# Seven-product weight sums, made in the second batch's up phase instead of the first batch's feed-forward part

## The chip, the cores and the metric

The kernel runs on one core of a Trainium2 chip. The metric is the device time of one execution in microseconds (us), the median of several. The engines are TensorE (PE, matmuls; its weight loads are listed as PEld), VectorE (DVE), ScalarE (ACT) and GpSimd (POOL). SyncE (SP) issues all DMA transfers, in the order of its queue.

## The reference

Attention with a window and block summaries, then a feed-forward part in which the tokens are first mixed by a matrix of rank 32. Cut to what matters:

```python
batch, heads, S, D = 4, 8, 768, 64           # DM = 512, hidden DF = 2048
a = softmax([scores in a window of 16 | scores with the block maxima of k])
x = a @ [v | block means of v]               # -> (4, 768, 512)
u = x + ((x^T @ U) @ V)^T                    # U (768, 32), V (32, 768)
out = u + relu(u @ w_ch1) @ w_ch2            # w_ch1 (512, 2048), w_ch2 (2048, 512)
```

All weights reach the chip as float64 bit patterns and are turned into float32 there.

## The kernel before, in words

**Precision.** A matmul operand is held as a high part (ACT casts it, L184) and a low part (the rest, by a subtraction on POOL, L185; a few on DVE), and a product is three matmuls: high by high, high by low, low by high. Casting and subtracting together are called a split.

**Order.** Every engine works through its own list of instructions in the order in which the program's text issues them, and so does SP with its transfers. The order is written by hand: attention steps of the next batch are spread between the matmuls of the present one.

**First batch** (from some 57 to 236 us; before that its attention). The loop at L1024 runs over the 16 blocks `f` of 128 hidden columns, in two token halves `hf`. Each half does 12 matmuls of the up product (L791), the relu into `gh`, `gl` (L803, L804), and 9 matmuls of the down product (L813). Beside that, weights two or three blocks ahead are loaded as 512 KB of float64 words, turned into float32 by POOL (L160) and DVE (L166, L169), and split. `traffic` issues the transfers of each quarter of a block. The float32 weights are stored to DRAM for the later batches (`store_up`, `store_down`). The first batch's result leaves through `leave_rows` (L826: copies out of PSUM on ACT and, for one of three, DVE), transposes on PE (L834) and additions on DVE (L837, L838).

**Later batches.** Each has an up phase (1061 to 1130) and a down phase. The up product goes by pairs `p` of hidden blocks with seven products in place of eight: the 2 x 2 blocks A11, A12, A21, A22 of the weights and four sums of them, S1 to S4, meet seven operands made of the activations. Of a pair, the products use A11, A12, A22 and the four sums, each block 128 x 256. PE runs seven products of six matmuls (L1066) a pair; results leave PSUM by copies on ACT (L1088, L1100, L1112, L1125) and additions on DVE (L1092, L1105, L1126, the last at a pair's end). Between them stand the attention steps of the next batch: matmuls L321 and L423, masked scores on DVE (L341, written as operations with an accumulator `neg`), exponentials on ACT (L351), the largest keys per block on DVE (L286, copied by L303), and a turn of the exponentials by way of DRAM (`squares`, `there`, `at`: L371, L376, L384).

**Weights of the later batches.** `fetch_weight` (L744) loads the next 512 or 384 KB from DRAM into one of three tiles (`whole`), `prepare` (L751) splits the next unit of it into one of eight tiles (`parts`). The units of a pair are A (A11, A12), S0 (s2, s1), S1 (s3, s4) and D (A22). Units are split one pair ahead of their use. `tick` runs once a step and starts a due load.

**The sums before.** `sum_weights` (L701) makes them in the first batch, in two halves at every even `f`, from the two float32 tiles of the pair: L709 and L710 give s1 and s2, L712 and L713 give s3 and s4, each 128 x 256 on DVE. `store_sums` stores them (512 KB a pair). `store_up` stores all of A11, A12 (256 KB) and of the other tile only A22 (128 KB).

Of the kernel before, what the change touches and what calls it, by code (L numbers as in the profile page):

```python
# [84 lines left out]
def body(ctx: ExitStack, tc, q0, q1, k, v, vn, uv, w1, w2, mask, ident, rep, out):  # L85
# [28 lines left out]
    def hidden_place(k, dt=F32):  # L114
        return wt.tile([P, 4 * NH], dt, name="place", tag=f"h{k}")
# [561 lines left out]
    def by_parts(val):  # L677

        return val.rearrange("p (i k f) -> p k i f", k=2, f=P)
# [14 lines left out]

    w_kept, w_sums = {}, {}
    up_there = [dram.tile([P, 14 * P], F32, name=f"up{p}", bufs=1) for p in range(NF // 2)]
    down_there = [dram.tile([P, 2, DM], F32, name=f"down{p}", bufs=1) for p in range(NF // 2)]

    def sum_weights(p, n):  # L701

        a1, a2 = by_parts(w_kept[2 * p]), by_parts(w_kept[2 * p + 1])
        if n == 0:
            w_sums[p] = hidden_place(p % 2)[:, : 8 * P]
        sums = w_sums[p].rearrange("p (b i f) -> p b i f", b=4, f=P)
        s2, s1, s3, s4 = (sums[:, b] for b in range(4))
        if n == 0:
            nc.vector.tensor_tensor(s1, a2[:, 0], a2[:, 1], ALU.add)  # L709
            nc.vector.tensor_tensor(s2, s1, a1[:, 0], ALU.subtract)  # L710
        else:
            nc.vector.tensor_tensor(s3, a1[:, 0], a2[:, 0], ALU.subtract)  # L712
            nc.vector.tensor_tensor(s4, a1[:, 1], s2, ALU.subtract)  # L713
# [12 lines left out]

    def store_sums(p):
        nc.sync.dma_start(out=up_there[p][:, 4 * P : 12 * P], in_=w_sums[p])

    loads, units = [], []
    for _ in range(1, B):
        for p in range(NF // 2):
            loads += [up_there[p][:, : 8 * P], up_there[p][:, 8 * P :]]
            units += [("A", p), ("S0", p), ("S1", p), ("D", p)]
        for p in range(NF // 2):
            loads.append(down_there[p].rearrange("p t c -> p (t c)"))
            units += [("down", 2 * p), ("down", 2 * p + 1)]
    load_tags = ("w2", "w0_1", "w0_2")  # L740
    unit_tags = ("w1_1", "w0_3", "w1_2", "w0_4", "w1_3", "w0_0", "w1_4", "w1_0")
    fetched, prepared, used, due = [], [], [], []

    def fetch_weight():  # L744
        n = len(fetched)
        if n < len(loads):
            t = wt.tile([P, 2 * DM], F32, name="whole", tag=load_tags[n % 3])[:, : loads[n].shape[-1]]
            nc.sync.dma_start(out=t, in_=loads[n])
            fetched.append(t)

    def prepare():  # L751

        n = len(prepared)
        if n == len(units):
            return
        key = units[n]
        second = key[0] in ("S0", "D") or key[0] == "down" and key[1] % 2 == 1
        whole = fetched[n // 2][:, DM:] if second else fetched[n // 2][:, :DM]
# [9 lines left out]
        prepared.append((key, t))  # L768
# [220 lines left out]
    def traffic(f, i):  # L989
# [7 lines left out]
                fetch_weight()  # L997
        if i == 1:
            store_down(f)
            if f % 2:  # L1000
                store_sums(f // 2)
            if f == NF - 2:
                prepare()
        if i == 2:
            if 1 < f and f + RING - 2 < NF:
                load_weight(1, f + RING - 2)
            if f == NF - 4:
                fetch_weight()
            if f == NF - 1:
                prepare()  # L1010
# [13 lines left out]
    for f in range(NF):  # L1024
        for hf in range(2):
# [3 lines left out]
            if hf == 0:  # L1029
                if 0 < f:  # L1030
                    split_weights(f + 1)
                if f % 2 == 0:
                    sum_weights(f // 2, 0)
            elif f + 3 <= NF:
                scale_weights(f + 3)
            sum_values(4 * f + 2 * hf)
            run(turn, hf)
            if hf == 1 and f % 2 == 0:
                sum_weights(f // 2, 1)
            if prev is not None:  # L1040
                pf, phf, pg = prev
                if pf == 0:
# [265 lines left out]
```

## Time and profile before

| | us |
|---|---|
| median of 3 runs | 681.97 |
| lowest and highest | 680.58, 685.45 |
| the profiled execution | 678.02 |
| its span, first to last instruction | 676.2 |

| in the span | PE | DVE | ACT | POOL |
|---|---|---|---|---|
| busy, us | 641.9 | 386.6 | 343.1 | 372.0 |
| share | 95% | 57% | 51% | 55% |

The span runs from the first to the last instruction; times in rows of the profile are counted from its start. A row of the timeline gives start, length, engine, line, operation, output and inputs, and in brackets how long the engine stood idle before it and what ended that. L12 is line 12 of the kernel. Names like `place` and `whole` are tiles; `place` is used for many. The first batch's attention takes up to some 57 us, its feed-forward part up to 236, the second batch's up phase up to 307 and its down phase up to 387.

### The profile page before, as it was taken

To read this page: it belongs to the slowest core of one execution; us is meant where nothing else is said; L and a number is where in the kernel's file an instruction comes from. 1 tells how busy PE (TensorE), PEld (TensorE's weight loads), DVE (VectorE), ACT (ScalarE), POOL (GpSimd) and SP (SyncE) were. 2 spreads that over 40 slices of the span, in tenths; PEclk is the share of its full clock that TensorE was granted. 3 is DMA by queue.
4 is the path that set the end of the run, shared out by engine and by line. 5 is a ranking of instruction groups with operands and counts; after the bars stand their busy time and mean duration, and the time that the engine had idled before them with its cause. 6 is when DMAs were issued, how large, how long until landed. Compare 5 with 4: busy or idle time off the path is not lost.

```text
span 676.2 us, 13190 instructions
## 1 busy us (share of the span) xinstructions
PE 641.9 (95%) x4800; PEld 568.2 (84%) x4800; DVE 386.6 (57%) x1041; ACT 343.1 (51%) x751; POOL 372.0 (55%) x428
## 2 busy tenths in 40 slices
PE   5889997989999899999999999999999999999997
PEld 4768796879888799998877899998877899998886
DVE  3778798777898666555655634566654432232222
ACT  3855356355433556665453467665543365553322
POOL 5846967635697757651245486661334375563420
PEclk9999999899999999999999999999999999999999
DMA  9999679898992169785438059777432144431002
GB/s 250 249 345 279 218 231 297 252 272 305 279 330 100 52 185 309 209 250 151 143 104 248 23 174 311 229 222 220 127 97 79 55 148 165 139 126 62 32 0 94
DMA packets 82752, 124.47 MB, mean 184 GB/s; under 512 B 7680, under 2 KB 57728, under 8 KB 82688
## 3 DMA queue, kind: packets, MB, share of 16 engines
q1 hardware_dynamic: 82688, 123.63, 60.3%
q8 instruction: 38, 0.62, 0.4%
q14 instruction: 26, 0.21, 0.1%
HBM read 96.34 MB, written 27.26 MB: 183 GB/s over the span
## 4 chain that ended last, share of the span: by engine, by line
PE 75%; DMA 11%; DVE 6%; ACT 3%; SPq 2%; POOL 2%; issue 1%; ACTq 0%; POOLq 0%; DVEq 0%
PE acc L1151 27%; PE ps_h L1066 24%; PE acc L813 7%; PE ps_h L791 6%; PE ps_s L321 4%; PE ps_x L423 3%; DMA place<-in_q 2%; DMA qz<-in_q 2%; PE ps_o L610 2%; DMA place<-in_w 1%; DMA at<-there 1%; DMA place<-in_v 1%; DVE gl L1136 1%; DMA kt<-in_k 1%; DMA place<-in_k 1%
## 5 line engine op out<-in xcount | busy, mean ns | idle before, releaser
L185 POOL TENSOR_TENSOR parts<-whole,parts 128x512 fp32r<-128x512 f32 (+1 forms) x144 | 181.6, 1270 | 165.6 <-ACT parts L184 137.1
L1151 PE MATMUL acc<-parts,gh 128*128 128x512 f32 x576 | 193.4, 399 | 0.0
L1066 PE MATMUL ps_h<-op,parts 128*128 128x384 f32 x1008 | 188.4, 339 | 1.2 <-POOL parts L185 0.6
L1066 PEld LDWEIGHTS ps_h<-op,parts 128*128 128x128 f32 x1008 | 173.6, 188 | 3.1 <-POOL parts L185 0.9
L1151 PEld LDWEIGHTS acc<-parts,gh 128*128 128x128 f32 x576 | 108.1, 188 | 22.9 <-issue 0.8
L1151 PE MATMUL acc<-parts,gl 128*128 128x512 f32 x288 | 113.1, 393 | 1.9 <-DVE gl L1136 1.9
L1136 DVE SCALAR_TENSOR_TENSOR gl<-place,gh 128x768 fp32r<-128x768 f32 x48 | 58.9, 1228 | 83.1 <-ACT gh L1135 83.0
L184 ACT CAST parts<-whole 128x512 fp32r<-128x512 f32 (+1 forms) x144 | 83.5, 583 | 5.8 <-DMA whole<-up 4.3
L351 ACT ACTIVATE e<-e,neg 128x120 f32<-128x120 f32 x144 | 46.5, 386 | 59.7 <-DVE neg L341 53.6
L791 PE MATMUL ps_h<-place 128*128 128x384 f32 x384 | 74.3, 341 | 1.2 <-DVE place L592 0.5
L813 PE MATMUL acc<-place,gh 128*128 128x512 f32 x192 | 68.3, 411 | 2.1 <-POOL place L185 2.1
L791 PEld LDWEIGHTS ps_h<-place 128*128 128x128 f32 x384 | 66.6, 188 | 4.2 <-DVE place L592 1.3
L1135 ACT ACTIVATE gh<-place 128x768 fp32r<-128x768 f32 x48 | 40.6, 846 | 55.1 <-PE acc L1151 54.9
L1151 PEld LDWEIGHTS acc<-parts,gl 128*128 128x128 f32 x288 | 54.2, 188 | 13.1 <-DVE gl L1136 3.9
L160 POOL TENSOR_SCALAR val<-place 128x512 f32<-128x512 f32 (+1 forms) x30 | 48.7, 1638 | 29.6 <-ACT place L147 17.7
L185 POOL TENSOR_TENSOR place<-val,place 128x512 fp32r<-128x512 f32 x29 | 38.6, 1351 | 19.5 <-ACT place L184 19.5
L185 POOL TENSOR_TENSOR op<-tmp,op 128x384 fp32r<-128x384 f32 x24 | 24.5, 1030 | 42.7 <-ACT op L184 38.5
L341 DVE CUSTOM_DVE_ANT_0 e<-ps_s,mask_sb 128x120 f32<-128x120 f32 x144 | 32.9, 278 | 25.3 <-PE ps_s L321 24.5
L813 PEld LDWEIGHTS acc<-place,gh 128*128 128x128 f32 x192 | 36.6, 192 | 11.1 <-POOL place L185 3.4
L803 ACT ACTIVATE gh<-ps_h 128x384 fp32r<-128x384 f32 x32 | 15.6, 488 | 54.3 <-PE ps_h L791 54.1
L321 PEld LDWEIGHTS ps_s<-kt,qz 128*128 128x128 f32 x288 | 39.0, 191 | 4.4 <-DVE kt L303 1.6
L321 PE MATMUL ps_s<-kt,qz 128*128 128x120 f32 x288 | 39.7, 274 | 2.0 <-DVE kt L303 1.2
(110 smaller groups left out, 848.4 us busy)
## 6 DMA issues: line engine op xcount, KB each, us to landing
place<-in_w SPq DMA_DIRECT2D x32, 512.0 KB, 6.0
whole<-up SPq DMA_DIRECT2D x24, 512.0 KB, 4.0
whole<-down SPq DMA_DIRECT2D x24, 512.0 KB, 3.7
there<-squares SPq DMA_DIRECT2D x24, 384.0 KB, 4.2
at<-there SPq DMA_DIRECT2D x96, 96.0 KB, 3.9
whole<-up SPq DMA_DIRECT2D x24, 384.0 KB, 3.5
vt<-in_v SPq DMA_DIRECT2D x48, 146.2 KB, 4.0
kt<-in_k SPq DMA_DIRECT2D x24, 288.0 KB, 5.6
```

Of the source, the lines that this page charges most:

```text
L160: nc.gpsimd.tensor_scalar(f32(bits), f32(hi), 0.0, None, ALU.mult)
L184: nc.scalar.copy(hi, val)
L185: engine.tensor_tensor(lo, val, f32(hi), ALU.subtract)
L321: nc.tensor.matmul(ps[:, i * KC : (i + 1) * KC], qt[:, 64 + j * P : 64 + j * P + P], kt[:, k0 : k0 + KC], start=True, stop=True,)
L341: nc.vector.tensor_tensor_reduce(out=e[:, i, :], in0=ps[:, i * KC : (i + 1) * KC], in1=mask_sb[:, m, :], scale=-SCALE, scalar=BIG, op0=ALU ...
L351: nc.scalar.activation(e[:, i, :], e[:, i, :], AF.Exp, bias=st.neg[h][:, u : u + 1], scale=-1.0,)
L791: nc.tensor.matmul(ps[:, :NH], w_split[0, f][:, c % 2, part_w, c // 2], ut[:, c, :], start=(n == 0), stop=(n == 3 * NC - 1),)
L813: nc.tensor.matmul(acc[t], gt[:, sl], w_split[1, f][:, part_w], start=(first and j == 0), stop=(last and j == 2),)
L1066: nc.tensor.matmul(ps, a[:, sa, i], b[:, sb, i], start=(first and n == 0), stop=(n == 5), skip_group_check=not first,)
L1135: nc.scalar.activation(gh, h, AF.Relu)
L1136: nc.vector.scalar_tensor_tensor(gl, h, 0.0, f32(gh), ALU.max, ALU.subtract)
L1151: nc.tensor.matmul(acc[t], gt[:, sl], w[:, part_w], start=(f == 0 and j == 0), stop=(f == NF - 1 and j == 2),)
```

## The change

The sums leave the first batch. `store_up` stores A21 as well, as a transfer of its own, and a pair's tile in DRAM grows from 14 to 16 blocks of 128 columns: A1, the place of the sums, A22, A21. In the second batch a pair's two loads become one load (`ends`: A1, A22, A21, 512 KB) and one making of sums on DVE from it, into the tile that the second load used. `sum_weights` is now a generator: two operations when it is begun, two more in the same step's `tick`, and two steps later the store of the sums. It is begun in the step in which the pair before has had its unit D split, and the next load follows three steps later. Pairs 0 and 1 are begun in the first batch's last blocks, pairs 2 to 7 in the second batch's up phase. The third and fourth batches load as before.

```diff
-    up_there = [dram.tile([P, 14 * P], F32, name=f"up{p}", bufs=1) for p in range(NF // 2)]
+    up_there = [dram.tile([P, 16 * P], F32, name=f"up{p}", bufs=1) for p in range(NF // 2)]
-    def sum_weights(p, n):
-        a1, a2 = by_parts(w_kept[2 * p]), by_parts(w_kept[2 * p + 1])
...
+    def sum_weights(p, whole, sums):
+        a1 = by_parts(whole[:, : 4 * P])
+        a22, a21 = (whole[:, 2 * i * P : 2 * (i + 1) * P].rearrange("p (k f) -> p k f", k=2) for i in (2, 3))
+        s2, s1, s3, s4 = (sums[:, 2 * i * P : 2 * (i + 1) * P].rearrange("p (k f) -> p k f", k=2) for i in range(4))
+        nc.vector.tensor_tensor(s1, a21, a22, ALU.add)
+        nc.vector.tensor_tensor(s2, s1, a1[:, 0], ALU.subtract)
+        yield
+        nc.vector.tensor_tensor(s3, a1[:, 0], a21, ALU.subtract)
+        nc.vector.tensor_tensor(s4, a1[:, 1], s2, ALU.subtract)
+        yield
+        yield
+        nc.sync.dma_start(out=up_there[p][:, 4 * P : 12 * P], in_=sums)
...
-            nc.sync.dma_start(
-                out=there[:, 12 * P :].rearrange("p (i f) -> p i f", f=P), in_=by_parts(w_kept[f])[:, 1]
-            )
+            for i in range(2):
+                o = (14 - 2 * i) * P
+                nc.sync.dma_start(
+                    out=there[:, o : o + 2 * P].rearrange("p (k f) -> p k f", k=2), in_=by_parts(w_kept[f])[:, i]
+                )
...
-            loads += [up_there[p][:, : 8 * P], up_there[p][:, 8 * P :]]
+            n = len(loads)
+            if n < NF:
+                ends = up_there[p].rearrange("p (a c) -> p a c", a=4)[:, ::3]
+                loads += [ends, p]
+                where = (n, 0), (n + 1, 0), (n + 1, 4 * P), (n, 4 * P)
+            else:
+                loads += [up_there[p][:, : 8 * P], up_there[p][:, 8 * P : 14 * P]]
...
     def fetch_weight():
...
+            if isinstance(loads[n], int):
+                stages.append(sum_weights(loads[n], fetched[n - 1], t))
+                next(stages[-1])
...
     def prepare():
...
-        if second:
+        if n < 2 * NF:
+            if n % 4 == 3:
+                due.extend((1, 4))
+        elif n % 2 == 1:
             due.append(4)
...
     def tick():
...
+        if stages:
+            for _ in stages[0]:
+                return
+            stages.pop(0)
...
     def traffic(f, i):
...
-            if f % 2:
-                store_sums(f // 2)
...
-            if f == NF - 4:
+            if f == NF - 3:
                 fetch_weight()
...
-                if f % 2 == 0:
-                    sum_weights(f // 2, 0)
...
-            if hf == 1 and f % 2 == 0:
-                sum_weights(f // 2, 1)
```

The lists of PE, ACT and POOL keep their order. On DVE and SP rows move. In the changed kernel lines below L696 have other numbers: the sums are L706, L707, L709 and L710, the relu's rest L827 (L804 before), the copy L849 (L826), the additions of the up phase L1109, L1122 and L1143 (L1092, L1105 and L1126).

DVE in the first batch, pair 1, before:

```order
L804 SCALAR_TENSOR_TENSOR gl<-ps_h,gh 128x384
L166 SCALAR_TENSOR_TENSOR val<-place,val 128x512
L712 TENSOR_TENSOR place<-val 128x256
L713 TENSOR_TENSOR place<-val,place 128x256
L169 SCALAR_TENSOR_TENSOR val<-place,val 128x512 x2
L804 SCALAR_TENSOR_TENSOR gl<-ps_h,gh 128x384
L286 TENSOR_REDUCE km<-kt 128x3x2 x2
L303 COPY kt<-km 64x4x12 x4
```

and of the change:

```order
L827 SCALAR_TENSOR_TENSOR gl<-ps_h,gh 128x384
L166 SCALAR_TENSOR_TENSOR val<-place,val 128x512
L169 SCALAR_TENSOR_TENSOR val<-place,val 128x512 x2
L827 SCALAR_TENSOR_TENSOR gl<-ps_h,gh 128x384
L286 TENSOR_REDUCE km<-kt 128x3x2 x2
L303 COPY kt<-km 64x4x12 x4
```

The two sums between the weights' turning (L166, L169) are gone, and the copies L303 follow on less work.

DVE at the end of the first batch, where the results leave PSUM, before (in brackets the engines waited for):

```order
L647 TENSOR_TENSOR tmp<-ps_o,tmp 128x384 [waits DVE_49,Pool_49]
L804 SCALAR_TENSOR_TENSOR gl<-ps_h,gh 128x384 [waits Activation_49]
L826 COPY r<-acc_907 128x512 [waits DMAHW5_49,PE_49]
L837 TENSOR_TENSOR o<-ps_o,place 128x384 [waits DMAHW4_49,PE_49]
L838 TENSOR_TENSOR o<-o,place 128x384 [waits DVE_49]
```

and of the change:

```order
L647 TENSOR_TENSOR tmp<-ps_o,tmp 128x384 [waits DVE_49,Pool_49]
L827 SCALAR_TENSOR_TENSOR gl<-ps_h,gh 128x384 [waits Activation_49]
L706 TENSOR_TENSOR whole<-whole 128x256 [waits DMAHW2_49,Pool_49]
L707 TENSOR_TENSOR whole<-whole 128x256 [waits DVE_49]
L709 TENSOR_TENSOR whole<-whole 128x256
L710 TENSOR_TENSOR whole<-whole 128x256 [waits DVE_49]
L849 COPY r<-acc_902 128x512 [waits DMAHW4_49,PE_49]
L860 TENSOR_TENSOR o<-ps_o,place 128x384 [waits DMAHW7_49,DMAHW6_49,PE_49]
L861 TENSOR_TENSOR o<-o,place 128x384 [waits DVE_49]
```

The four sums of pair 1 stand ahead of the copy, and the first of them waits for POOL.

DVE in the second batch's up phase, at a pair's end, of the change:

```order
L371 STREAM_TRANSPOSE squares<-e 128x768 [waits Activation_49,Pool_49]
L1143 TENSOR_TENSOR place<-place,ps_h 128x384 [waits Activation_49]
L706 TENSOR_TENSOR whole<-whole 128x256 [waits DMAHW3_49,Pool_49]
L707 TENSOR_TENSOR whole<-whole 128x256 [waits DVE_49]
L709 TENSOR_TENSOR whole<-whole 128x256
L710 TENSOR_TENSOR whole<-whole 128x256 [waits DVE_49]
L1122 TENSOR_TENSOR place<-place,ps_h 128x384 [waits PE_49,Activation_49]
L341 ISA e,neg<-ps_s,mask_sb 128x120 [waits PE_49]
```

Before, L1126 was followed there by L1105 at once. The sums stand between the last addition of one pair and the first of the next, with the masked scores behind them.

More of the change, by code (lines that the diff above doesn't have):

```diff
@@ L693, in split_weights @@
             w_split[i, f] = t
-    w_kept, w_sums = {}, {}
-    up_there = [dram.tile([P, 14 * P], F32, name=f"up{p}", bufs=1) for p in range(NF // 2)]
+    w_kept = {}
+    up_there = [dram.tile([P, 16 * P], F32, name=f"up{p}", bufs=1) for p in range(NF // 2)]
     down_there = [dram.tile([P, 2, DM], F32, name=f"down{p}", bufs=1) for p in range(NF // 2)]
-    def sum_weights(p, n):
-        a1, a2 = by_parts(w_kept[2 * p]), by_parts(w_kept[2 * p + 1])
[L704 to L713, printed above, removed]
+    def sum_weights(p, whole, sums):
[10 more added lines that the diff above has]
+        nc.sync.dma_start(out=up_there[p][:, 4 * P : 12 * P], in_=sums)
     def store_up(f):
@@ L742, in body @@
     fetched, prepared, used, due = [], [], [], []
+    stages = []
     def fetch_weight():
@@ L746, in fetch_weight @@
         if n < len(loads):
-            t = wt.tile([P, 2 * DM], F32, name="whole", tag=load_tags[n % 3])[:, : loads[n].shape[-1]]
-            nc.sync.dma_start(out=t, in_=loads[n])
+            t = wt.tile([P, 2 * DM], F32, name="whole", tag=load_tags[n % 3])
             fetched.append(t)
+            if isinstance(loads[n], int):
+                stages.append(sum_weights(loads[n], fetched[n - 1], t))
+                next(stages[-1])
+            elif len(loads[n].shape) == 3:
+                nc.sync.dma_start(out=t.rearrange("p (a c) -> p a c", a=2), in_=loads[n])
+            else:
+                nc.sync.dma_start(out=t[:, : loads[n].shape[-1]], in_=loads[n])
     def prepare():
@@ L755, in prepare @@
             return
-        key = units[n]
-        second = key[0] in ("S0", "D") or key[0] == "down" and key[1] % 2 == 1
-        whole = fetched[n // 2][:, DM:] if second else fetched[n // 2][:, :DM]
+        *key, load, col = units[n]
+        whole = fetched[load][:, col : col + (2 * P if key[0] == "D" else DM)]
         t = wt.tile([P, 2 * DM], F32R, name="parts", tag=unit_tags[n % 8])[:, : 2 * whole.shape[-1]]
@@ L767, in prepare @@
         split(hi, lo, whole, nc.gpsimd)
-        prepared.append((key, t))
-        if second:
+        prepared.append((tuple(key), t))
+        if n < 2 * NF:
+            if n % 4 == 3:
+                due.extend((1, 4))
+        elif n % 2 == 1:
             due.append(4)
```

7 lines of the change are left out of this document (3 added, 4 removed).

## The prediction

> **What bounds the kernel now.** I read the busy time by stage first, since the share over the whole span mixes stages with different limits. Columns: length of the stretch, then busy time of TensorE (PE), its weight loads, VectorE (DVE), ScalarE (ACT) and GpSimd (POOL), the granted clock, the share of the DMA engines and GB/s.
>
> ```profile
> core 0: us, PE busy (x) PEld busy (x) DVE busy (x) ACT busy (x) POOL busy (x), PEclk, DMA share, GB/s
> 57.00:236.00 179.00, 166.72 (x1258) 146.16 (x1259) 140.56 (x341) 84.41 (x184) 125.17 (x128) 0.98 0.76 236
> 95.00:115.00 20.00, 18.18 (x145) 15.95 (x143) 18.92 (x64) 13.29 (x32) 13.27 (x17) 1.00 0.99 306
> 236.00:307.00 71.00, 70.46 (x556) 68.48 (x555) 43.98 (x153) 44.81 (x106) 43.82 (x55) 1.00 0.80 239
> ```
>
> 57 to 236 us is the first batch's feed-forward part, which the sums leave; 236 to 307 is the second batch's up phase, which they enter. PE is the bound in both, but differently. In the first it stands idle for 12.3 us, DVE is 79% busy, and in places DVE and the DMA engines are full. In the second PE is idle for 0.5 us and DVE for 27.0 us. So a gain can only come out of PE's idle time in the first, and a loss comes where DVE runs late in the second. What ends PE's waits in the first stage (total us, times, longest; three shorter rows left out):
>
> ```profile
> PE ps_x L423 <- DMA at<-there: 3.8, 2, 3.7
> PE acc L813 <- POOL place L185: 2.1, 3, 0.9
> PE ps_o L834 <- DVE r L826: 1.3, 1, 1.3
> PE ps_x L423 <- DVE val L166: 1.2, 1, 1.2
> PE ps_s L321 <- DVE kt L303: 1.2, 1, 1.2
> PE ps_s L321 <- DVE neg L341: 0.8, 1, 0.8
> PE ps_m L537 <- DVE gl L804: 0.7, 1, 0.7
> PE ps_o L610 <- DVE x L605: 0.6, 1, 0.6
> ```
>
> No engine's total matters here: these eight rows (11.7 us) are the stock from which the change can draw.
>
> **What leaves the first batch.** The four lines that make the sums, by groups (busy us, mean ns):
>
> ```profile
> L709 DVE TENSOR_TENSOR place<-val 128x256 f32<-128x256 f32 x8 | 5.5, 688 | 0.0
> L710 DVE TENSOR_TENSOR place<-place,val 128x256 f32<-128x256 f32 x8 | 5.5, 685 | 0.3
> L712 DVE TENSOR_TENSOR place<-val 128x256 f32<-128x256 f32 x8 | 5.4, 680 | 0.0
> L713 DVE TENSOR_TENSOR place<-val,place 128x256 f32<-128x256 f32 x8 | 4.4, 549 | 0.0
> ```
>
> 32 operations, 20.8 us, 0.65 us each. Eight of them (pairs 0 and 1) stay in this stage, at its end, so DVE loses about 15.6 us net. Most of this hides nothing but DVE's own slack. It counts where a sum stands in an unbroken row of DVE work that a PE wait ends on:
>
> ```profile
> 77.72 0.54 DVE L712 TENSOR_TENSOR place<-val 128x256 f32<-128x256 f32 x1
> 78.18 0.96 DVE L713 TENSOR_TENSOR place<-val,place 128x256 f32<-128x256 f32 x1
> 100.52 0.86 DVE L712 TENSOR_TENSOR place<-val 128x256 f32<-128x256 f32 x1
> 101.31 0.41 DVE L713 TENSOR_TENSOR place<-val,place 128x256 f32<-128x256 f32 x1
> 210.38 1.53 DVE L709 TENSOR_TENSOR place<-val 128x256 f32<-128x256 f32 x1
> 211.95 1.39 DVE L710 TENSOR_TENSOR place<-place,val 128x256 f32<-128x256 f32 x1
> ```
>
> The first two (1.4 us) stand before the L303 copies on which PE waits 1.2 us; the next two (1.2 us) before the L341 on which it waits 0.8; the last two (2.9 us) before the L605 on which it waits 0.6. Each removal is longer than its wait, so all three go: 1.2 + 0.8 + 0.6 = **2.6 us**. Of the waits on L166 and L804 (1.9 us), behind which sums stand only further back, I take a third: **0.6 us**. POOL's 2.1 us I leave.
>
> Beside DVE, the stores change (KB each, us to landing):
>
> ```profile
> up<-place SPq DMA_DIRECT2D x8, 512.0 KB, 5.2
> up<-val SPq DMA_DIRECT2D x8, 128.0 KB, 4.3
> ```
>
> Eight stores of 512 KB leave SyncE's (SP's) queue (one comes back near the stage's end, seven in the second batch), and eight of 128 KB, each an issue of its own, join the present eight: 2.6 MB less in this stage. The longest PE wait of the stage is a DMA chain in which such a store is ahead:
>
> ```profile
> 107.35 0.44 SPq L728 DMA_DIRECT2D up<-place x1
> 108.34 0.32 SPq L376 DMA_DIRECT2D there<-squares x1
> ```
>
> The squares' round trip through DRAM starts 1 us behind a 512 KB store, in the stretch with a DMA share of 0.99. At that stretch's 306 GB/s the store is 1.7 us of transfer, so the 3.7 us wait shrinks to about 2.0: **1.7 us**. What stands behind that wait is slow too, here against the same work elsewhere, by the chain that ended last (start, us):
>
> ```profile
> 117.66 1.53 PE ps_x L423 x48
> 119.19 3.95 PE acc L813 x9
> 125.89 2.08 PE acc L813 x9
> 152.12 0.89 PE ps_x L423 x48
> ```
>
> Half-speed work cost 0.64 + 1.87 = 2.5 us after this one long wait, and none after the waits of 1.2 us and less. Whether a wait of 2.0 us still triggers it no row shows, so I count half: **1.2 us**. (The Trainium skill, "TensorE: Matmul & The Clock Gate", section "What's actually happening", has the array fall to half clock after an idle window of about 3.4 us. The 3.7 us wait agrees. By that rule 2.0 us would not do it, and the sum below would be 1.3 us lower.)
>
> First stage: 2.6 + 0.6 + 1.7 + 1.2 = **6.1 us** off. Bounds: 0, if each wait is only replaced by the next; 11.7 + 2.5 less POOL's 2.1 and L826's 1.3 = 10.8 at most.
>
> **The end of the first batch.** The sums of pair 1 now stand ahead of the copy L826 that clears a PSUM bank, and wait for POOL, which must have read the tile they overwrite:
>
> ```profile
> 226.82 0.75 POOL L185 TENSOR_TENSOR parts<-whole,parts 128x256 fp32r<-128x256 f32 x1
> 226.90 0.69 DVE L826 COPY r<-acc 128x512 f32<-128x512 f32 x1 [0.92 <-PE acc L813]
> 229.44 1.48 PE L834 MATMUL ps_o<-ident_sb,r 128*128 128x128 f32 x12
> ```
>
> POOL is done at 227.6; four sums of 0.65 end at 230.2, the copy at 230.9. PE turns these rows from 229.4 and wants the copied one for its second transpose, at 229.5: it waits **1.4 us**. Behind the copy wait the eight additions L837/L838, and then PE's next wait on L826, which move by the same amount, not by more. Bounds: 0, if the first batch's end gets POOL earlier, and 3.
>
> **What enters the second batch.** The sums of pairs 2 to 7, 24 operations, come behind the last addition L1126 of each weight pair, again behind POOL's split of block A22:
>
> ```profile
> 274.65 0.56 DVE L1126 TENSOR_TENSOR place<-place,ps_h 128x384 f32<-128x384 f32 x1 [0.90 <-ACT place L1125]
> 275.57 0.74 POOL L185 TENSOR_TENSOR parts<-whole,parts 128x256 fp32r<-128x256 f32 x1
> ```
>
> DVE is free at 275.2, POOL done at 276.3: 1.1 us of waiting, and 4 x 0.65 = 2.6 of work, 3.7 us for each of six pairs, 22 us against 27.0 idle. It fits, but DVE becomes 93% occupied and late within a pair. Queued behind a waiting sum are the additions L1105 and the masked scores L341, for which ACT's exponentials wait, and behind these on ACT the copies that PE's next product on the same bank needs. The nearest row is a delay of ACT of that size:
>
> ```profile
> 255.93 0.62 ACT L184 CAST parts<-whole 128x512 fp32r<-128x512 f32 x1 [2.18 <-DMA whole<-up]
> 258.92 3.24 PE L1066 MATMUL ps_h<-op,parts 128*128 128x384 f32 x17 [0.54 <-ACT place L1125]
> ```
>
> 2.2 us late on ACT cost PE 0.5 us. DVE's spare time is 27.0 / 8 = 3.4 us a pair, about half of it ahead of those exponentials, so ACT is 3.7 - 1.7 = 2.0 us late where one follows directly. I take that for six pairs in ten: 0.3 us of PE a pair, **1.8 us**. The two rows also give a gain: the load that ACT waits for there holds s3 and s4, which are now made on the core from blocks that an earlier load brought, so this **0.5 us** goes.
>
> On SP the wait for POOL moves away:
>
> ```profile
> SPq L748 <- POOL parts L185: 17.9, 7, 3.5
> ```
>
> Now the loads stand behind POOL's splits and hold up SP; of the pair's two, the one that is left overwrites a tile whose splits are long done. The new stores of the sums are issued two steps behind the operations, with DVE done or nearly. I cost SP at nothing either way, as PE waits for no DMA in this stage. Bounds for the stage: -0.5, and +9.7 (below). The third and fourth batches read the same 512 and 384 KB as before: nothing.
>
> What a sum takes when POOL works beside it:
>
> ```profile
> 58.82 0.41 DVE L709 TENSOR_TENSOR place<-val 128x256 f32<-128x256 f32 x1
> 210.35 2.72 POOL L185 TENSOR_TENSOR place<-val,place 128x512 fp32r<-128x512 f32 x2
> ```
>
> It took 0.41 us at 58.82 and 1.53 at 210.38, under the first of POOL's two splits. (The Trainium skill, "SBUF — State Buffer", section "Who interferes with whom", has a rule that speaks against this change: a DVE operation with two SBUF inputs and a POOL operation that reads SBUF shut each other out for a whole instruction. The trace agrees with it here.) What it can come to in the second batch is the third rival.
>
> **Sum.** -6.1 + 1.4 + 1.8 - 0.5 = -3.4 us. The profiled execution took 678.0 us (span 676.2), so 674.6 for such a one. The median of the runs is 682.0, 4 us above the profiled one; on that scale the forecast is **678.6 us**. About 1%, 6.8 us, is what a measurement of this kernel tells from no change.
>
> **The rivals.**
> - *The first stage gives everything* (0.20): 10.8 us, with the same costs: -8.1, 673.9. For it: DVE carries 79% there, and 2.6 MB fewer pass through DMA engines that are full for long stretches. Against it: the waits on POOL's splits stay, and SP's queue is issued in the same order.
> - *The first stage gives next to nothing* (0.22): the stage runs as its transfers arrive, and each wait passes to the next load. With 2 us gained: -2 + 2.7 = +0.7, 682.7. For it: the chain holds several DMA pieces in this stage. Against it: three of the eight waits end on DVE right behind a sum.
> - *DVE becomes the bound of the second up phase* (0.13): on the other side. POOL runs a split or an addition in 62% of that stage; if each sum takes the 1.53 us of the row at 210.38, DVE needs 44.0 + 24 x 1.53 = 80.7 us in 71, 9.7 more. It decides from a mean of 27.0 / 24 = 1.1 us a sum. Sum: -6.1 + 1.4 + 9.7 - 0.5 = +4.5, 686.5; with the second rival's first stage, 690.6.
>
> The forecast keeps 0.45. Faster by over 1% (below 675.2) is nearly all of the first rival and a little of the forecast: 0.24. Slower by over 1% (above 688.8) is half of the third and little else: 0.09. Within 1%: 0.67. The range holds all but the far ends of the first and third: 671 to 687.
>
> **What would show it.** In the changed profile: DVE's busy time in the first feed-forward part 13 to 19 us lower, and no PE wait on L303 or L605 there; the long wait on the squares' return about 2 us, with or without the slow clock behind it; a new PE wait of about 1.4 us on the copied rows at the change of batches; in the second up phase sums of 0.6 to 0.8 us behind POOL's split, and PE idle some 2 us instead of 0.5. Wrong would be: sums above 1.1 us, a new long DMA wait in the first part, or PE waits there on POOL that grow as others go.

## The result, and the profile after

The changed kernel takes 683.38 us (median of 20 runs, 680.43 to 687.43), the kernel before 679.25 us in the same comparison (20 runs, 675.96 to 685.45): ratio 1.0068, 95% interval 1.0053 to 1.0084. That is 4.6 us slower, where the forecast was 3.4 us faster. The profiled execution of the change took 685.31 us (span 683.5), that of before 678.02 (span 676.2).

Where the stages end is read from the timeline: the first row of PE in which the second batch's up product runs, and the first of its down product. Before:

```profile
230.67 1.64 PE L1066 MATMUL ps_h<-op,parts 128*128 128x384 f32 x8
300.55 0.39 PE L1151 MATMUL acc<-parts,gh 128*128 128x512 f32 x1
```

After:

```profile
226.33 3.40 PE L1083 MATMUL ps_h<-op,parts 128*128 128x384 f32 x18
307.88 0.39 PE L1168 MATMUL acc<-parts,gh 128*128 128x512 f32 x1
```

The first batch ends 4.3 us earlier, and the second up phase takes 81.5 us in place of 69.9. Everything behind it keeps its time. (The prediction's bounds of these stages, 57, 236 and 307 us, lie 4 to 6 us behind these rows.) In the table, us, by such rows; the columns are the first batch's attention, its feed-forward part, the second batch's up and down phase, and the rest:

| kernel | attention | first feed-forward | second up | second down | rest |
|---|---|---|---|---|---|
| before | 52.9 | 177.8 | 69.9 | 85.8 | 289.8 |
| after | 51.3 | 175.0 | 81.5 | 85.9 | 289.8 |

The first two columns differ by 3 to 4 us from one profile to the next. The second up phase varies too: in three profiles without any sums in it, and with its loads at the times of before, it took 69.9, 70.6 and 72.8 us (the last two are runs of the last group of experiments). So the columns are used below with the times, not by themselves. The same windows as in the prediction, moved with these rows (length, then PE, weight loads, DVE, ACT, POOL, clock, DMA share, GB/s):

```profile
57.00:231.60 174.60, 164.07 (x1251) 144.12 (x1250) 124.43 (x314) 83.83 (x184) 122.25 (x128) 0.99 0.73 221
231.60:314.30 82.70, 75.28 (x556) 71.92 (x555) 60.62 (x177) 44.17 (x106) 44.62 (x55) 0.96 0.77 225
```

DVE's busy time in the first stage fell by 16.1 us, from 140.6 to 124.4, as the sums left. In the second it rose by 16.6, and is still only 73% of a stretch that has grown. So DVE is not full; it is late. What ended PE's waits in the second stage, where before there were 0.5 us in one wait (a row of 0.8 us is left out):

```profile
PE ps_x L423 <- DMA at<-there: 3.6, 2, 1.9
PE ps_h L1083 <- ACT place L1129: 3.0, 3, 2.1
```

And what ACT waits for, before:

```profile
ACT e L351 <- DVE neg L341: 7.7, 8, 1.8
ACT parts L184 <- DMA whole<-up: 2.2, 1, 2.2
```

and after:

```profile
ACT e L351 <- DVE neg L341: 19.9, 8, 5.1
ACT parts L184 <- DMA whole<-up: 6.7, 4, 2.9
```

The exponentials wait 12.2 us longer for the masked scores, and the casts 4.5 us longer for a load. Who is late on whom shows in one pair of hidden blocks, by the timeline (SP, DVE, ACT and PE rows put together):

```profile
261.56 0.33 SPq L713 DMA_DIRECT2D up<-whole  x1
262.01 0.38 SPq L763 DMA_DIRECT2D whole<-up  x1
267.57 0.43 DVE L706 TENSOR_TENSOR whole<-whole 128x256 f32<-128x256 f32 x1 [2.01 <-DMA whole<-up]
268.37 1.48 DVE L709 TENSOR_TENSOR whole<-whole 128x256 f32<-128x256 f32 x1
269.78 0.95 DVE L710 TENSOR_TENSOR whole<-whole 128x256 f32<-128x256 f32 x1
270.76 0.34 SPq L713 DMA_DIRECT2D up<-whole  x1
271.12 0.27 DVE L341 CUSTOM_DVE_ANT_0 e<-ps_s,mask_sb 128x120 f32<-128x120 f32 x1
271.19 1.58 SPq L763 DMA_DIRECT2D whole<-up  x1
271.43 0.97 ACT L351 ACTIVATE e<-e,neg 128x120 f32<-128x120 f32 x3 [3.34 <-DVE neg L341]
273.75 0.46 ACT L1129 COPY place<-ps_h 128x384 f32<-128x384 f32 x1
274.26 4.91 PE L1083 MATMUL ps_h<-op,parts 128*128 128x384 f32 x18 [2.06 <-ACT place L1129]
279.66 3.38 PE L1083 MATMUL ps_h<-op,parts 128*128 128x384 f32 x18
```

This is a ring. A load (L763, at 262.01) stands in SP's list behind a store of sums (L713, 261.56). The sums of the next pair wait for that load (L706 at 267.57, 2.01 us), the store of these sums can only leave at 270.76, and the next load stands behind it again (271.19). A turn takes 9.2 us. SP's own waits in the second stage say the same: 16.6 us in four waits for the sums.

```profile
SPq L713 <- DVE whole L710: 16.6, 4, 6.5
```

On DVE the sums stand ahead of the masked scores L341. While they wait and run, ACT waits 3.34 us for the scores; the copy L1129 stands behind the exponentials; PE waits 2.06 us for the copy, and then does 18 matmuls in 4.91 us that take 3.38 us five us later: the clock is down (the granted clock is 0.50 from 275.8 to 277.5 us and 1.00 from 279.6 on). So one late load costs PE 2.06 + 1.53 us.

### The profile page after: what moved, and what is told of

Its sections match the earlier page's. It is cut to its first block, busy times and chain, and to the rows that moved or that the text cites. A ratio compares the mean times of both kernels' runs of the same rounds, so it can differ in the third digit from the quotient of the medians.

```text
span 683.5 us, 13181 instructions
## 1 busy us (share of the span) xinstructions
PE 645.8 (94%) x4800; PEld 571.2 (84%) x4800; DVE 388.0 (57%) x1041; ACT 342.1 (50%) x751; POOL 370.4 (54%) x428
## 4 chain that ended last, share of the span: by engine, by line
PE 67%; DMA 11%; DVE 7%; POOL 5%; ACT 3%; SPq 3%; issue 2%; ACTq 0%; POOLq 0%; DVEq 0%
PE acc L1168 26%; PE ps_h L1083 21%; PE acc L836 5%; PE ps_h L814 4%; PE ps_s L321 4%; PE ps_x L423 2%; DMA whole<-up 2%; DMA at<-there 2%; POOL val L160 2%; DMA place<-in_v 2%; PE ps_o L610 2%; DMA place<-in_q 1%; DMA kt<-in_k 1%; DVE gl L1153 1%; POOL place L185 1%
## 5 line engine op out<-in xcount | busy, mean ns | idle before, releaser
L1083 PE MATMUL ps_h<-op,parts 128*128 128x384 f32 x1008 | 192.5, 344 | 4.5 <-ACT place L1129 3.0
L1083 PEld LDWEIGHTS ps_h<-op,parts 128*128 128x128 f32 x1008 | 176.5, 191 | 7.7 <-ACT place L1129 4.2
L160 POOL TENSOR_SCALAR val<-place 128x512 f32<-128x512 f32 (+1 forms) x30 | 47.0, 1584 | 29.8 <-ACT place L147 29.6
L341 DVE CUSTOM_DVE_ANT_0 e<-ps_s,mask_sb 128x120 f32<-128x120 f32 x144 | 32.8, 278 | 23.7 <-PE ps_s L321 23.1
L826 ACT ACTIVATE gh<-ps_h 128x384 fp32r<-128x384 f32 x32 | 15.6, 489 | 52.9 <-PE ps_h L814 52.7
```

What stands on the lines that cost most here:

```text
L160: nc.gpsimd.tensor_scalar(f32(bits), f32(hi), 0.0, None, ALU.mult)
L341: nc.vector.tensor_tensor_reduce(out=e[:, i, :], in0=ps[:, i * KC : (i + 1) * KC], in1=mask_sb[:, m, :], scale=-SCALE, scalar=BIG, op0=ALU ...
L1083: nc.tensor.matmul(ps, a[:, sa, i], b[:, sb, i], start=(first and n == 0), stop=(n == 5), skip_group_check=not first,)
```

## The experiments

Each ratio is against the kernel before, run on the same chip beside it (median 679.0 to 680.0 us there).

### The order of store and load on SP

The ring is opened from two sides: the store of the sums two steps later, behind the load (first edit), or the load two steps earlier, ahead of the store (second edit). The third leaves the store out.

```diff
         yield
         yield
+        yield
+        yield
         nc.sync.dma_start(out=up_there[p][:, 4 * P : 12 * P], in_=sums)
```

> The changed kernel, with the store of a pair's sums issued two steps later, so that the next load stands ahead of it on SP and no longer waits for DVE's last sum; nothing else moves. Queue theory (in the second up phase load, sums, store and next load form a ring, since SP is in order): the waits of ACT and DVE on the load (11.3 us in the second up phase of the changed kernel) fall below 4 us, the stage is 5 to 9 us shorter, and the time comes down from 683.4 to 675 to 679. Port theory (DVE is late because POOL's operations stretch the sums from 0.4 to 1.5 us): the ring is only a symptom, the time stays within 2 us of the changed kernel, 681 to 685. Tile theory (DVE is late because the sums wait for POOL to have read the tile they overwrite): also 681 to 685.

```diff
-                due.extend((1, 4))
+                due.extend((1, 2))
```

> The changed kernel, with the next load started one step after the sums are begun instead of three: it too stands ahead of the store, and is also two steps earlier, behind POOL's split of S1 instead of behind DVE. Queue theory: as good as moving the store or better, 674 to 678, with next to no wait of DVE or ACT on the load. Port and tile theories: 681 to 685, and DVE waits on POOL in place of the load.

```diff
     def sum_weights(p, whole, sums):
...
-        yield
-        yield
-        nc.sync.dma_start(out=up_there[p][:, 4 * P : 12 * P], in_=sums)
...
     def store_up(f):
...
+            nc.sync.dma_start(out=there[:, 4 * P : 8 * P], in_=w_kept[f])
+            nc.sync.dma_start(out=there[:, 8 * P : 12 * P], in_=w_kept[f])
```

> The changed kernel without the stores of the sums in the second batch; so that their place in DRAM holds something, the first batch stores A11, A12 there twice (two more transfers of 256 KB a pair), and the third and fourth batches use these numbers in place of the sums. Queue theory: the second up phase is as short as with the store moved, 72 to 75 us instead of 83, and the first batch's part about 1 us longer than in the changed kernel. Transfer theory (it is the store's traffic, not its place in the queue, that makes the loads late): the stage is shorter here but not with the store moved. Port and tile theories: the stage stays at 80 us and more.

Measured: 681.25 us, ratio 1.0014 (0.9990 to 1.0039); 680.01 us, 1.0012 (0.9990 to 1.0035); 680.63 us, 1.0016 (0.9995 to 1.0037). The second up phase took 76.3, 76.0 and 74.5 us. All three give the same: some 0.55% of the time, 3.7 us, was the order of two transfers in SP's list. The traffic of the store does not show, as leaving it out gives no more than moving it; the third kernel stores 4 MB more in the first batch, though, so its time alone would not prove it. Its phase is 1.5 us shorter than the second kernel's, less than such profiles differ by. In the second of them ACT waits for no load any more, but still long for the scores:

```profile
ACT e L351 <- DVE neg L341: 17.9, 7, 5.7
```

So the queue theory is right and not enough: 6.1 us over the phase of before are left.

### What a sum takes, and what stands behind it

Three theories for the rest: DVE and POOL shut each other out in the sums (port); the first sum waits for POOL's split of A22, whose tile it overwrites (tile); or only the length of the DVE work ahead of the scores counts (order). All kernels here build on the one with the earlier load.

```diff
-        nc.vector.tensor_tensor(s1, a21, a22, ALU.add)
+        nc.vector.tensor_reduce(s1, a21.unsqueeze(3), AX.X, ALU.max)
... (s2, s3, s4 alike)
```

> The sums become operations of the same shape that read one input from SBUF instead of two (a maximum over an axis of length one), so the numbers are not the sums; everything else is as in e2_load_two_steps_earlier, whose second up phase took 76.0 us against 69.9 before. Port theory (a sum of 0.76 us on average, 0.41 alone, because POOL and DVE shut each other out): the sums fall to about 0.4 us, POOL's splits under them are no longer held up, the second up phase falls to 71 to 72 us, and the time to about 676. Tile theory (the first sum waits for POOL's split of A22, whose tile it overwrites): the wait stays, the sums are shorter, the phase falls by at most 2 us, to 74 to 75. Plain order theory (2 to 3 us of DVE work ahead of the masked scores, however it runs): between these, in proportion to the DVE time, some 18.3 - 24 x 0.41 = 8.5 us less of it, 1.4 us a pair.

Measured: 672.84 us, ratio 0.9905 (0.9883 to 0.9927); second up phase 69.5 us, below what any of the three theories had. Groups of the four operations in that phase (busy us, mean ns), with the two inputs:

```profile
L706 DVE TENSOR_TENSOR whole<-whole 128x256 f32<-128x256 f32 x6 | 5.9, 978 | 4.7 <-POOL parts L185 4.0 <-DMA up<-whole 0.6
L709 DVE TENSOR_TENSOR whole<-whole 128x256 f32<-128x256 f32 x6 | 4.8, 798 | 0.0
L707 DVE TENSOR_TENSOR whole<-whole 128x256 f32<-128x256 f32 x6 | 4.5, 749 | 0.2
L710 DVE TENSOR_TENSOR whole<-whole 128x256 f32<-128x256 f32 x6 | 3.1, 521 | 0.0
```

and with one:

```profile
L707 DVE TENSOR_REDUCE whole<-whole 128x256 f32<-128x256 f32 x6 | 2.5, 420 | 0.2
L706 DVE TENSOR_REDUCE whole<-whole 128x256 f32<-128x256 f32 x6 | 2.5, 419 | 4.3 <-POOL parts L185 4.2
L709 DVE TENSOR_REDUCE whole<-whole 128x256 f32<-128x256 f32 x6 | 2.5, 409 | 0.0
L710 DVE TENSOR_REDUCE whole<-whole 128x256 f32<-128x256 f32 x6 | 2.5, 409 | 0.0
```

18.3 us of sums became 10.0, 0.41 to 0.42 us each whatever POOL does beside them. The wait for POOL's split stayed (4.2 us), and with short operations behind it, it cost next to nothing. But is it POOL being held up, or DVE's time? The same four operations, each issued twice, give DVE as much to do as the sums:

```diff
-        nc.vector.tensor_reduce(s1, a21.unsqueeze(3), AX.X, ALU.max)
+        for _ in range(2):
+            nc.vector.tensor_reduce(s1, a21.unsqueeze(3), AX.X, ALU.max)
... (s2, s3, s4 alike)
```

> e4_one_input_sums with every one of the four operations issued twice: 48 operations of 0.41 us in the second up phase and the first batch's end, so 3.3 us of DVE work a pair, as much as the sums took in e2_load_two_steps_earlier (3.05 us), and none of it shutting POOL out (the numbers are not the sums). If only the DVE time ahead of the masked scores counts, the phase is back at 75 to 76 us and the time at 679 to 680. If the hold on POOL's splits counts as well, it stays at 71 to 73 us, and 673 to 675.

Measured: 683.07 us, ratio 1.0069 (1.0043 to 1.0096); second up phase 76.5 us. PE waits for the copy again, and ACT for the scores:

```profile
PE ps_h L1087 <- ACT place L1133: 5.2, 4, 2.3
```

```profile
ACT e L351 <- DVE neg L341: 21.8, 7, 6.0
```

By the phase (76.5 us against 76.0) 3.3 us of such work a pair ahead of the scores cost what the sums cost, and by the time 0.6% more; 1.65 us cost nothing that shows (69.5 us, against 69.9 without sums). POOL's splits of 128x512 took 1.36 us on average in the phase with the sums and 1.33 in that with the doubled operations, so POOL was hardly held up. What is left for the port is that a sum takes 0.76 us and not 0.41. (The Trainium skill, "SBUF — State Buffer", section "Who interferes with whom", names `tensor_reduce` as an operation that never meets GpSimd's port on this chip, and `tensor_tensor` with both inputs in SBUF as one that does. The two groups above agree: 0.41 to 0.42 us against 0.52 to 0.98.)

The tile theory by itself, and a kernel that makes the sums on POOL:

```diff
-            t = wt.tile([P, 2 * DM], F32, name="whole", tag=load_tags[n % 3])
+            if isinstance(loads[n], int):
+                t = hidden_place((0, 2, 4, 5, 6, 7, 6, 7)[loads[n]])[:, : 8 * P]
+            else:
+                t = wt.tile([P, 2 * DM], F32, name="whole", tag=load_tags[n % 3])
```

> e2_load_two_steps_earlier with the sums written to a tile that nothing else uses at that time, in place of the one that POOL's split of A22 and S0, S1 have just read. Tile theory: DVE's wait on POOL ahead of the first sum (4.0 us in two waits) goes, and the second up phase falls from 76.0 to 72 to 73 us. Port theory and plain order theory: the four sums stand at the same place on DVE and take the same time or longer, since they now begin while POOL is still splitting; the phase stays at 75 to 77 us and the time at 680.

```diff
-        nc.vector.tensor_tensor(s1, a21, a22, ALU.add)
+        nc.gpsimd.tensor_tensor(s1, a21, a22, ALU.add)
... (s2, s3, s4 alike)
```

> e5_sums_own_tile with the sums made on POOL instead of DVE. POOL took 0.74 us for a 128x256 subtraction, so 24 more cost it 17.8 us, and it would be busy some 62 us of the second up phase. Port theory and plain order theory: nothing is left ahead of the masked scores on DVE, and the phase falls to 70 to 72 us, the time to some 675; if POOL itself comes late with its splits, PE waits on parts appear and the phase is 74 or more. Tile theory: no lower than e5_sums_own_tile.

Measured: 676.95 us, ratio 0.9958 (0.9932 to 0.9984), second up phase 73.4 us, and 678.31 us, 0.9984 (0.9960 to 1.0009), 73.9 us. The wait for POOL's tile is worth 3 to 4 us by the times when two-input sums stand behind it (2.6 by the phases), as the tile theory had it, and not the 0 that the port and order theories gave it. So the order theory needs a correction: not the length of the work alone counts, but how long DVE is held at the sums, waiting and working, before it comes to the scores. The sums in their own tile are the longest of all, 19.7 us in the phase, 3.3 a pair like the doubled operations, but nothing is waited for ahead of them (0.2 us), and the kernel is 6 us faster by the medians than that with the doubled ones. Held for 14.5 us (one-input operations), the ratio is 0.9905; for 19.9 (own tile), 0.9958; for 23.1 to 23.3 (the three kernels of the group before), 1.0012 to 1.0016; for 25.8 (doubled) and 26.5 (the change), 1.0069 and 1.0068. That is a reading across runs, not an experiment that steps the time for which DVE is held.

On POOL the sums are 20 us of work, and the exponentials wait no longer for the scores than before (7.0 us). PE waits for POOL's splits instead, and longer than before (1.3 us) for the copied rows at the phase's start:

```profile
PE ps_h L1086 <- POOL parts L185: 1.1, 1, 1.1
PE ps_o L860 <- DVE r L852: 2.3, 1, 2.3
```

Behind the second wait 12 matmuls took 3.89 us, in place of 2.33 in the change.

Last the sums on DVE, in a tile of their own, but one in each of four steps instead of all in one:

```diff
         nc.vector.tensor_tensor(s1, a21, a22, ALU.add)
+        yield
         nc.vector.tensor_tensor(s2, s1, a1[:, 0], ALU.subtract)
         yield
         nc.vector.tensor_tensor(s3, a1[:, 0], a21, ALU.subtract)
+        yield
         nc.vector.tensor_tensor(s4, a1[:, 1], s2, ALU.subtract)
...
                 stages.append(sum_weights(loads[n], fetched[n - 1], t))
-                next(stages[-1])
```

> e5_sums_own_tile with the four sums of a pair put one into each of four steps in a row instead of all into one, so that never more than one stands ahead of a masked score or an addition. If what is left of the loss is a burst of 2.6 to 4 us of DVE work in front of the scores that ACT waits for, the second up phase falls from 73.4 to 70 to 71 us, and the time from 677.0 to 674 to 675. If what is left is the time that DVE and POOL take from each other, wherever the sums stand, the phase stays at 73 us and the time at 677.

Measured: 674.11 us, ratio 0.9948 (0.9918 to 0.9977); second up phase 69.1 us, as short as without sums. This version is faster than both kernels. From 232 to 302 us (columns as above) PE has no wait at all, and ACT's longest wait for the scores is 1.8 us, as in the kernel before:

```profile
232.00:302.00 70.00, 70.00 (x554) 68.16 (x554) 58.00 (x177) 44.83 (x107) 46.29 (x55) 1.00 0.80 250
```

Its sums took 16.6 us, hardly less than in the change. By the ratios it is not told apart from the version with the sums in one step (0.9958), as the intervals overlap. The profiles do not settle it: the 73.4 us are from an execution 3.4 us above its kernel's median, and are some 4 us longer by one stall of PE and the slow clock behind it. A profile without any sums (the second of the next group, 72.8 us) has such a stall too, where 24 matmuls took 4.46 us in the kernel before. The two rows, own tile first:

```profile
273.28 4.96 PE L1086 MATMUL ps_h<-op,parts 128*128 128x384 f32 x18 [2.17 <-ACT place L1132]
256.91 6.02 PE L1076 MATMUL ps_h<-op,parts 128*128 128x384 f32 x24 [1.88 <-ACT place L1135]
```

What the times do show is that with one sum a step, the load ahead and a tile of its own, no cost of the sums is left that can be measured: 674.11 us, against 674.78 without sums (next group).

### The first part by itself

The sums and their stores are taken out of the first batch and made nowhere.

> The first half of the change alone: the sums are made nowhere. All later batches load A11, A12, A22, A21 (512 KB) and, in place of the sums, 512 KB of down weights from DRAM, so their products use other numbers. If the first batch's gain is what the two profiles show (2.7 us), and the rest of the loss is the second batch's, this takes 675 to 678 against 679.3 before. By the prediction's 6.1 us it would be 672 to 674. If the first batch gives nothing, 679 to 681.

Measured: 691.05 us, ratio 1.0157 (1.0133 to 1.0181). This one says nothing of the question: it began the loads of all later batches when the last split of a pair was issued, and the part behind the second batch took 302.3 us in place of 289.8. With the loads at their times of before:

```diff
-            if n < NF:
-                ends = up_there[p].rearrange("p (a c) -> p a c", a=4)[:, ::3]
-                loads += [ends, p]
...
+            ends = up_there[p].rearrange("p (a c) -> p a c", a=4)[:, ::3]
+            loads += [ends, down_there[p].rearrange("p t c -> p (t c)")[:, : 6 * P]]
...
+        if n % 2 == 1:
             due.append(4)
```

> The first part of the change alone: the sums and their stores are gone from the first batch and made nowhere; the second batch loads 512 and 384 KB a pair in the places and at the times of the kernel before, and blocks of other weights stand in for the sums. Only the numbers differ, not the work of the later batches. The forecast's step for the first stage: 6.1 us less in the first batch (4.7 with the end's cost, which is not paid here), so some 674 against 680. What the profile of the change suggests: the first stage gives 2.8 us and perhaps the 1.0 to 1.4 of its end, 676 to 677, with the second up phase at 69.9 as before. Second rival of the forecast: 678.

and the same with the sums made in the first batch as before (`sum_weights` as in the kernel before), but not stored:

```diff
+                if f % 2 == 0:
+                    sum_weights(f // 2, 0)
...
+            if hf == 1 and f % 2 == 0:
+                sum_weights(f // 2, 1)
```

> e6b_first_part_alone with the four sums made in the first batch at their places of before and stored nowhere: only the stores of the sums are missing from the first batch (other weights stand in for them later). It parts the first stage's gain (4.2 us in e6b_first_part_alone) into DVE's work and the transfers. By the forecast's terms: the transfers' share is 1.7 + 1.2 = 2.9 of 6.1 us, so this would be at some 677 against 674.8 there and 679.0 before. If all of the gain is DVE's work: 679. If all of it is the transfers: 675.

Measured: 674.78 us, ratio 0.9940 (0.9919 to 0.9961), and 675.26 us, 0.9963 (0.9937 to 0.9989). So the first part by itself gains 4.1 us (2.6 to 5.5), and of these 2.5 us (0.7 to 4.3) come with the sums still on DVE, from the missing stores alone. What DVE's work adds is 1.6 us by the ratios and 0.5 by the medians, and not told from nothing. The profile of the second shows the three DVE waits of the prediction back, 2.5 us together, though its median is only 0.5 us longer (rows between these left out):

```profile
PE ps_x L423 <- DMA at<-there: 3.9, 2, 3.2
PE ps_s L321 <- DVE kt L303: 1.1, 1, 1.1
PE ps_s L321 <- DVE neg L341: 0.8, 1, 0.8
PE ps_o L610 <- DVE x L605: 0.6, 1, 0.6
```

## Why the prediction was wrong, step by step

The forecast was 3.4 us less, 678.6 us, on a scale on which the kernel before takes 682.0 (three runs; twenty gave 679.25). That the measured 683.38 lie inside its range of 671 to 687, and next to the second rival's 682.7, is luck. The direction was wrong, and that rival adds 2 us off in the first stage and 2.7 on behind it, where the runs show 4.1 off and 8.7 on: 4.6 us slower in all, with a first part that gains 4.1 by itself.

**The reading of the bounds** was right as far as it went: PE idles in the first stage, a gain comes from there, and a loss from a late DVE in the second.

**First stage, 6.1 us: 4.1 by itself.** What ended PE's waits of the change in this stage:

```profile
PE ps_x L423 <- DMA at<-there: 4.7, 3, 2.9
PE ps_o L857 <- DVE r L849: 2.0, 2, 1.3
PE acc L836 <- POOL place L185: 1.2, 2, 0.8
PE ps_s L321 <- DVE kt L303: 1.0, 1, 1.0
```

"Each removal is longer than its wait, so all three go" failed for L303. The waits on L341, L605 and L166 went. But ahead of the copies L303 DVE now idles for the relu of PE's product:

```profile
78.42 0.56 DVE L827 SCALAR_TENSOR_TENSOR gl<-ps_h,gh 128x384 fp32r<-128x384 f32 x1 [0.93 <-ACT gh L826]
79.53 1.39 DVE L303 COPY kt<-km 64x48 f32<-64x48 f32 x4
80.97 0.93 PE L321 MATMUL ps_s<-kt,qz 128*128 128x120 f32 x6 [1.03 <-DVE kt L303]
```

The 1.4 us of sums were taken out of an idle that another engine sets; only what reaches back without a gap to the wait counts. And a PE wait that goes is a gain only if PE then isn't held elsewhere: the DMA waits grew from 3.8 us in two to 4.7 in three. The run without the stores puts the whole DVE term, forecast at 3.2 us (2.6 + 0.6), at 0.5 by the medians and 1.6 by the ratios, with intervals too wide to tell it from nothing or from 3.2.

**The wait on the squares, 1.7 us, and the clock, 1.2 us:** the long wait fell from 3.7 to 2.9 us, so 0.8, and work behind it stayed slow (granted clock 0.50 from 115.4 to 117 us).

```profile
114.62 0.93 PE L423 MATMUL ps_x<-vt,at 120*32 120x65 f32 x48 [2.89 <-DMA at<-there]
```

The sum of both, 2.9, is close to the 2.5 that the stores are worth over the whole stage, but that is luck: with the stores gone and the sums kept, the long wait is still 3.2 us.

**End of the first batch, 1.4 us:** a new wait of 0.76 us on the copied rows. POOL was done with its split 1.9 us ahead of PE's first transpose, as before; but the four sums took 2.2 us instead of 2.6, two of them 0.41 each, the copy followed at once, and PE came 0.2 us later to the copied rows. Inside its bounds.

```profile
225.15 1.42 PE L857 MATMUL ps_o<-ident_sb,r 128*128 128x128 f32 x11 [0.76 <-DVE r L849]
```

**Second up phase, +1.8 and −0.5: measured +11.6. This is where the forecast fell,** in three steps. The 11.6 us are of one profiled execution, 1.9 us above its kernel's median; by the times, all that the second part adds, the first batch's end included, is 8.7 us, where the forecast had 2.7.

1. "I cost SP at nothing either way, as PE waits for no DMA in this stage." The store was looked at by itself, with DVE "done or nearly". What is queued behind it on SP, the next pair's load, was not followed on, nor that its data are now wanted two links earlier: by DVE's sums, not only by ACT's casts. A ring of load, sums, store and load was the result, and 3.7 us. For the same reason the 0.5 us of gain didn't come: the waits for the load went from one of 2.2 us to four with 6.7. And PE does wait for DMA in this stage now, 3.6 us in two waits on the squares' return: in both cases the transposition L371 that starts their turn stands behind a pair's sums on DVE.
2. "2.2 us late on ACT cost PE 0.5 us", taken for six pairs in ten: 0.3 us a pair. The delay itself was forecast well: 3.7 us a pair of waiting and sums, and with the load ahead it was 3.9 (23.2 us in the phase). The spare time ahead of the scores, 1.7 us, was put too low if anything: 2.4 us a pair (the one-input operations with their waits) cost nothing that shows. What failed is the price of what goes beyond it. With the load ahead, the phase was still 6.1 us longer than before, 1.0 us a pair (0.8 by the times, against the first part by itself), and with 4.3 us a pair (the doubled operations) 6.6 us longer. One row with a cover of its own was taken as the price of all.
3. The clock behind a stall was counted in the first stage only. In the second, the stall of 2.06 us shown above is followed by 18 matmuls of 4.91 us in place of 3.38, and so is another:

```profile
302.24 0.89 PE L423 MATMUL ps_x<-vt,at 120*32 120x65 f32 x48 [1.95 <-DMA at<-there]
303.05 4.99 PE L1083 MATMUL ps_h<-op,parts 128*128 128x384 f32 x18
```

Together 3.1 us of the 11.6.

The mean of a sum was as forecast, 0.74 us (17.7 us for 24), and the waits for POOL were two, with 4.0 us, where six of 1.1 were forecast; 4.6 us of waits for the load came on top. **The third rival** is not what happened, though the time came out near its side: no mean of 1.1 us, and DVE was not full (60.6 of 82.7 us). Its warning that the sums meet POOL was right, and its threshold, stated as a share of DVE's time, was the wrong measure. **Later batches, nothing:** right, 85.8 and 289.8 us before, 85.9 and 289.8 after.

What stays open: how the 4.1 us of the first stage are spread over its waits, as profiles of it differ by as much from one execution to the next; and for the same reason, how the cost behind the ring is split between the wait for POOL's tile and the length of the burst.

## What to carry to other kernels

When a step becomes a producer for later loads, follow the issuing queue past it: a store that waits for compute holds every load behind it, and if that compute waits for a load, the queue has closed a ring; put the load ahead. Price work that is added to an engine with idle time by what is queued behind it and how long it holds that in one piece, its own waits included, not by the engine's share: the same 17 us of sums cost 8 to 9 us by the times in bursts behind late loads and a busy tile, and nothing that could be measured with the load ahead, a tile of their own and one operation a step. And remove an engine's work for gain only where it reaches without a gap to a wait that PE ends on, and where PE has no transfer to wait for next.

## What the runs showed of the hardware

The granted clock falls after shorter waits than expected, and not after each. From the version with the load two steps earlier (each bracket is the wait):

```profile
115.40 0.89 PE L423 MATMUL ps_x<-vt,at 120*32 120x65 f32 x48 [2.18 <-DMA at<-there]
116.22 0.50 PE L836 MATMUL acc<-place,gh 128*128 128x512 f32 x1
280.89 3.27 PE L1083 MATMUL ps_h<-op,parts 128*128 128x384 f32 x12 [1.94 <-ACT place L1129]
```

After 2.18 us the work ran at full speed (granted clock 1.00 from 116.2 to 118 us); after 1.94 us 12 matmuls took 3.27 us (0.50 from 282.5 to 284.2), where in the run with doubled operations 12 took 2.38 us after a wait of 2.25 (1.00):

```profile
284.05 2.38 PE L1087 MATMUL ps_h<-op,parts 128*128 128x384 f32 x12 [2.25 <-ACT place L1133]
```

So no length of wait decides it here. (The Trainium skill, "TensorE: Matmul & The Clock Gate", section "What's actually happening", has the clock fall after at least one idle window of about 3.4 us, and the window run free of the kernel. The free-running window goes with a result that changes from stall to stall; the length does not, as waits of 1.88 to 2.06 us, shorter than the window, were enough.)
